# Attention before two expert layers on one core: the first pairs' maxima for both heads at once, and the reciprocal's correction inside the bank of the sums

## The chip, the cores and the metric

The kernel runs on one core of a Trainium2 chip. The metric is the device time of one execution in microseconds (us); the time of a kernel is the median of its runs. A profile is one further execution, recorded by the hardware profiler. Engines: PE is TensorE (matmuls), DVE is VectorE, ACT is ScalarE, POOL is GpSimd, SP issues most of the DMAs. PSUM is the memory that PE writes, in banks; SBUF is the working memory.

## What is computed

Three stages follow each other: attention over 4 x 8 heads (1152 positions, head size 64; the queries are first averaged in pairs, which leaves 576), a layer with `g = h*cos(h)`, and a layer with eight experts, one of which is chosen for each token. Only attention matters here:

```python
q_pool = q.reshape(B, H, S // factor, factor, D).mean(axis=3)
scores = scale * np.matmul(q_pool, k.transpose(0, 1, 3, 2))
scores = scores - np.max(scores, axis=-1, keepdims=True)
attn = np.exp(scores)
attn = attn / (np.sum(attn, axis=-1, keepdims=True) + 1e-09)
return np.matmul(attn, v).astype(np.float32)
```

## The kernel before

Attention works on 16 pairs of heads; the two heads of a pair lie on partitions 0 to 63 and 64 to 127. The queries of a pair are handled in two halves (`hq`) of 288, the keys in nine blocks (`j`) of 128. For every pair these steps run:

- `load`, `loadv`: DMAs of queries, keys and values. `qadd` (L248) adds neighbouring queries, on POOL. `kh`, `qh`, `qt` (L254 to L264, ACT) make rounded copies for the maxima.
- The maxima. `mx` (L273, L276) multiplies a tile of 128 queries (`t` = 0 to 3, and the last 64 queries of both heads as `t` = 4) by a third of the keys (`g`), for both heads at once, into one PSUM tile of two halves; `red` (L302, L305, DVE) reduces both halves in one instruction. There are 14 such tiles in a pair, and one buffer for them (the pool "x"; at the very start two more are lent by the scores' pool). For the second part of pair 0 (tiles `t` = 3 and 4) and for all of pair 1 the kernel does it in another way: `mx1` (L285, L287) fills one half of a tile that stays, in turn the first and the second half, and `red1` (L296) reduces that half.
- `mneg` (L314) joins the thirds and negates, `pmr` (L319) transposes, `mrow` (L324) copies, `mset` (L331, L333) puts the result into the rows `MR` by four DMAs. For the first part of pair 0 `pmq` (L340) and `mput` (L343) do that without a DMA.
- The scores. `s` (L349, L351) computes one block's scores with the maximum taken off, for both heads; `exp` (L355, ACT) takes their exponentials; `es` (L362, POOL) adds up the nine exponentials of a half, eight additions; `pv` (L368) multiplies by the values.
- The end of a half. `ob` (L372) copies the output out of PSUM, negated; `sum` (L377) sums the exponentials over the keys into a bank of PSUM; `ln` (L381) and `rcp` (L385), both on ACT, make a first reciprocal `r0` as exp(-ln(sum)); `nr1` (L389) and `nr2` (L392), both on DVE, correct it by one step: nr = (sum + 1e-9)*r0, then (nr - 2)*r0. `norm` (L400, POOL) multiplies.

Beside these run 32 conversions of weights for the next stage: `cload`, `cabs` (L413, ACT), `c1` to `c4` (L417 to L426, DVE), `chi` (L430, ACT), `clo` (L433, DVE), `cst`. They work in the pool "m", a single PSUM bank, which the transposed maxima and the sums use too, one after the other.

The order is not that of loops. `steps` lists every step with a wished time in units (a pair is 6 units), an engine, a cost, what it reads and writes, and a buffer; `plan` then builds the order of all five queues: it runs through simulated time and always takes, among the steps that an engine may take next (those wished for no later than `AHEAD` units after its first open one), the one with the least sum of its wished time, `WAIT` times its wait, and `SWITCH` when PE would change between its two layouts. For two buffers in turn it only knows what `steps` says: `mx1` waits there for the reduction of its own half alone. The kernel is then issued in the planned order, each engine's queue in that order.

Of the kernel before, what the change touches and what calls it, by code (L numbers as in the profile page):

```python
# [8 lines left out]
F32 = mybir.dt.float32  # L9
# [19 lines left out]
AHEAD = {"PE": 4.5, "DVE": 3.78, "ACT": 3, "POOL": 3.61, "SP": 8.0}  # L29
CHANGE = {COLS: 0.2, ROWS: 0.1}  # L30
EARLY = 4
BEHIND = 1.54
SPREAD = 5.1
WAIT, SWITCH = 6.04, 0.85


def steps(NP, NJ, J):


    P, nx = [], 0  # L40
# [5 lines left out]
    for i in range(NP):  # L46
        b = 6*i
        first = i == 0
        p = -101 if first else b - 10.75
# [8 lines left out]
        for x in whole:  # L58
            c = ((0.67, 0.33)[x] if first else 1)
            at(p + -0.49 + 9*x, "qadd", (i, x), "DVE" if first and not x else "POOL", 1.45*c, [("qr", i, x)] + [("q", i, 0)]*x, [("q", i, x)], None if x else ("q", 3, ("q", i, 0)))  # L60
            at(p + 0.1 + 9*x, "qh", (i, x), "ACT", 0.2 + 0.47*c, [("q", i, x)] + [("qh", i, 0)]*x, [("qh", i, x)], None if x else ("qh", 2, ("qh", i, 0)))
# [3 lines left out]
        at(-4 if first else p + 0.98, "qt", (i,), "ACT", 0.48, [("q", i, whole[-1])], [("qt", i % 2)])  # L65
        parts = ((0, 3), (3, 5)) if first else ((0, 5),)
        for lo, hi in parts:
            p = (-4 if lo else -100) if first else b - 8.47
            for n, (t, g) in enumerate(tiles):
                if lo <= t < hi:  # L70
# [5 lines left out]
                    if lo or i == 1:  # L76
                        for h in range(2) if t < 4 else (0, 1)[:3-g]:
                            half = ("x", nx % 2)
                            at(x, "mx1", (i, t, g, h, nx % 2), ROWS, 0.19, ks + [("xe",)]*(nx > 0), [half] + [("xe",)]*(nx == 0), None if nx else ("x", 1, ("xe",)))
                            at(x, "red1", (i, t, g, h, nx % 2), "DVE", 0.56, [half, ("xe",)], [("mx", i, lo)])  # L80
                            nx += 1
                        continue
                    at(x, "mx", (i, t, g), ROWS, 0.35 if (t, g) == (4, 0) else 0.19, ks, [key], ("s", 2, key) if p == -100 and n % 3 else ("x", 1, key))
                    at(x + 0.08, "red", (i, t, g), "DVE", 0.56 if (t, g) == (4, 2) else 0.96, [key], [("mx", i, lo)])
# [10 lines left out]
        for hq in range(2):  # L95
            for j in range(J):
# [4 lines left out]
                at(m + 0.17, "exp", key, "ACT", 0.65, [("s", *key)], [("e", *key)], ("e", 14, ("e", *key)))  # L101
                if j:
                    at(m + 0, "es", key, *(("DVE", 0.8) if (i, hq) == (NP-1, 1) and j > 4 else ("POOL", 1.45)), [("e", *key)] + [("e", i, hq, 0)]*(j == 1), [("es", i, hq)], ("es", 2, ("es", i, hq)) if j == 1 else None)
                at(m + BEHIND, "pv", key, COLS, 0.486, [("v", i), ("e", *key)], [("o", i, hq)], ("o", 1, ("o", i, hq)) if j == 0 else None)
            m = b + 3*hq + max(3.9, BEHIND + 2.7)
            key = (i, hq)
            at(m + -0.11, "ob", key, "ACT", 0.41, [("o", *key)], [("ob", *key)], ("ob", 2, ("ob", *key)))
            at(m + 0.1, "sum", key, COLS, 0.486, [("es", *key)], [("sum", *key)], ("m", 1, ("sum", *key)))
            at(m + 0.5, "ln", key, "ACT", 0.5, [("sum", *key)], [("ln", *key)], ("ln", 2, ("ln", *key)))
            at(m + 0.46, "rcp", key, "ACT", 0.44, [("ln", *key)], [("r0", *key)], ("r0", 2, ("r0", *key)))  # L110
            at(m + 0.3, "nr1", key, "DVE", 0.46, [("sum", *key), ("r0", *key)], [("nr", *key)], ("nr", 2, ("nr", *key)))
            at(m + 0.6, "nr2", key, "DVE", 0.46, [("r0", *key)], [("nr", *key)])
            at(m + 0.54, "norm", key, "POOL", 0.95, [("nr", *key), ("ob", *key)], [("xT", *key)])
    for n in range(NJ):
        x = 10.76 + 3.01*n if n < 27 else 89 + 1.2*(n - 27)
        at(x - 5, "cload", (n,), "SP", 0.6, (), [("ct", n)], ("ct", 2, ("ct", n)))
        at(x, "cabs", (n,), "ACT", 0.65, [("ct", n)], [("ca", n)], ("m", 1, ("ca", n)))
        for c in range(1, 5):
            at(x + 0, f"c{c}", (n,), "DVE", 0.69, [("ct", n)], [("ca", n)])
        at(x + 0.27, "chi", (n,), "ACT", 0.58, [("ca", n)], [("co", n)], ("co", 2, ("co", n)))  # L120
# [66 lines left out]
def attention(nc, tc, q, k, v, xT, ident, w_in, w_out, ws, x2d, W1):  # L187
# [11 lines left out]
    with ExitStack() as ctx:  # L199
# [78 lines left out]
        def mx1(i, t, g, h, b):  # L278

# [745 lines left out]
```

## Time and profile before

| | us |
|---|---|
| median of 3 runs (1231.37 to 1232.37) | 1232.14 |
| the profiled execution | 1230.01 |
| its span, first to last instruction | 1228.3 |
| PE busy | 1189.6 (97%) |
| DVE busy | 891.7 (73%) |
| ACT busy | 764.0 (62%) |
| POOL busy | 469.1 (38%) |

Busy time is the time in which an engine executes instructions; PE's ends are modelled, so a PE that counts as busy need not be at its peak. POOL's work lies almost wholly in the first 490 us, which is attention; in the later stages PE is the engine that is nearly always busy. The granted TensorE clock is 0.998 on average. The rows below name an instruction by its line, its engine and its tiles, as output<-inputs.

### The profile page before, as it was taken

The numbers are of one execution on the slowest core, as the hardware profiler recorded it, in microseconds if no ns is written. First come the engines' busy times: TensorE is split into PE (matmuls) and PEld (weight loads), VectorE is DVE, ScalarE is ACT, GpSimd is POOL, SyncE is SP. The second block draws the span as 40 slices with busy tenths as digits, with TensorE's granted clock in tenths as the row PEclk, the third lists the DMA queues.
The fourth block names the chain that finished last, engine by engine and source line by source line (L and its number), as shares of the span: only waits on it lengthen the run. The fifth ranks groups of instructions, "written<-read, shape, count | busy, mean of one in ns | idle before, by whom it ended". The sixth has DMA issues, their size and how long they took to land. (4 is left out here: it accounts for less than half of the span.)

```text
span 1228.3 us, 22291 instructions
## 1 busy us (share of the span) xinstructions
PE 1189.6 (97%) x8158; PEld 932.2 (76%) x8158; DVE 891.7 (73%) x1916; ACT 764.0 (62%) x1528; POOL 469.1 (38%) x414
## 2 busy tenths in 40 slices
PE   4799999999999999999999999999999999999997
PEld 2466666666666556989898889889987888888886
DVE  4568887887788767777767767767777877777761
ACT  2266666666666667666566565565575877677751
POOL 2489999999999886000000000000003121112100
PEclk9999999999999999999999999999999999999999
DMA  6034466434433236600000000000047997889710
GB/s 256 18 94 127 157 220 209 152 128 146 143 127 108 89 115 245 259 19 1 18 19 1 19 1 18 19 1 18 26 160 252 398 319 265 273 274 308 265 56 6
DMA packets 70942, 163.73 MB, mean 133 GB/s; under 512 B 7669, under 2 KB 24813, under 8 KB 68784
## 3 DMA queue, kind: packets, MB, share of 16 engines
q1 hardware_dynamic: 66832, 150.92, 35.5%
q0 software_dynamic: 4000, 11.38, 2.6%
q8 instruction: 64, 1.05, 0.3%
q14 instruction: 46, 0.38, 0.1%
HBM read 135.65 MB, written 28.39 MB: 134 GB/s over the span
## 5 line engine op out<-in xcount | busy, mean ns | idle before, releaser
L362 POOL TENSOR_TENSOR es<-es,E 128x576 f32<-128x576 f32 x220 | 313.7, 1426 | 27.4 <-ACT E L355 14.9
L355 ACT ACTIVATE E<-s 128x576 f32<-128x576 f32 x288 | 183.2, 651 | 109.6 <-PE s L351 102.2
L897 PE MATMUL h<-xh,wf 128*128 128x256 f32 x1152 | 231.9, 285 | 0.1
L918 PE MATMUL po<-wf,g 128*128 128x512 f32 x864 | 222.3, 394 | 1.3 <-ACT g L909 0.6
L302 DVE TENSOR_REDUCE MX<-pmx 128x2 f32<-128x768 f32 x177 | 168.7, 956 | 55.8 <-PE pmx L273 55.7
L754 POOL DMA_INDIRECT xg<-x2d,idx x25 | 26.9, 1075 | 465.5 <-ACT ar L902 388.8
L349 PE MATMUL s<-Q,K 64*128 64x288 f32 x1152 | 193.8, 419 | 1.5 <-ACT E L355 1.5
L897 PEld LDWEIGHTS h<-xh,wf 128*128 128x128 f32 x1152 | 188.1, 191 | 6.6 <-issue 1.8
L918 PEld LDWEIGHTS po<-wf,g 128*128 128x128 f32 x864 | 153.4, 189 | 28.1 <-ACT g L909 1.3
L743 DVE TENSOR_TENSOR w<-raw,w 128x1024 fp32r<-128x1024 f32 x128 | 154.6, 1220 | 22.2 <-ACT w L742 20.2
L897 PE MATMUL h<-xl,wf 128*128 128x256 f32 x576 | 163.2, 283 | 0.0
L368 PE MATMUL o<-E,vt 128*64 128x288 f32 x1152 | 161.2, 414 | 0.0
L351 PE MATMUL s<-MR,ON 64*128 64x288 f32 x576 | 148.5, 508 | 0.0
L742 ACT CAST w<-raw 128x1024 fp32r<-128x1024 f32 x128 | 132.9, 1052 | 20.5 <-DMA raw<-in_moe_w_dram 11.9
L821 PE MATMUL po<-w,hh 128*128 128x512 f32 x600 | 144.4, 393 | 1.0 <-DVE hh L792 0.6
L821 PEld LDWEIGHTS po<-w,hh 128*128 128x128 f32 x600 | 110.5, 188 | 24.1 <-DVE hh L792 1.5
L906 ACT ACTIVATE ar<-ar 128x256 f32<-128x256 f32 x144 | 60.1, 417 | 96.7 <-DVE ar L905 96.3
L368 PEld LDWEIGHTS o<-E,vt 128*64 128x64 f32 x1152 | 75.2, 136 | 58.2 <-issue 15.3
L349 PEld LDWEIGHTS s<-Q,K 64*128 64x128 f32 x1152 | 96.6, 187 | 25.8 <-ACT E L355 11.5
L897 PEld LDWEIGHTS h<-xl,wf 128*128 128x128 f32 x576 | 110.0, 191 | 3.7
L788 PE MATMUL ph<-xh,w 128*128 128x256 f32 x576 | 109.7, 287 | 1.0 <-ACT xh L715 1.0
L825 POOL DMA_INDIRECT out_dram<-ob,idx x25 | 27.2, 1090 | 201.9 <-ACT ob L824 183.8
(204 smaller groups left out, 1849.2 us busy)
## 6 DMA issues: line engine op xcount, KB each, us to landing
raw<-in_moe_w_dram SPq DMA_DIRECT2D x128, 512.0 KB
wf<-ws SPq DMA_DIRECT2D x16, 1024.0 KB
vt<-in_v_dram SPq DMA_DIRECT2D x16, 576.0 KB
qr<-in_q_dram SPq DMA_DIRECT2D x15, 576.0 KB
K<-in_k_dram SPq DMA_DIRECT2D x15, 576.0 KB
cv_t<-in_moe_w_in_dram SPq DMA_DIRECT2D x16, 512.0 KB
ws<-cv_o SPq DMA_DIRECT2D x32, 256.0 KB
cv_t<-in_moe_w_out_dram SPq DMA_DIRECT2D x16, 512.0 KB
```

The lines of the kernel that those rows point to most:

```text
L302: nc.vector.reduce_max(out.rearrange("p (w g) -> p w g", g=3)[:, 2*t:2*t+2, g], p[:, :, :KG], axis=AX.X)
L349: nc.tensor.matmul(p[:, h, :NQ], lhsT=T["k", i][R[h], j*128:(j+1)*128], rhs=T["q", i][R[h], qs], start=True, stop=False)
L351: nc.tensor.matmul(p[:, h, :NQ], lhsT=ON[R[h]], rhs=MR[i % 3][R[h], qs], start=False, stop=True)
L355: nc.scalar.activation(e, T.pop(("s", i, hq, j))[:, :, :NQ], AF.Exp, scale=1.0/16)
L362: (nc.vector if (i, hq) == (NP-1, 1) and j > 4 else nc.gpsimd).tensor_add(T["es", i, hq], T["e", i, hq, 0] if j == 1 else T["es", i, hq], ...
L368: nc.tensor.matmul(T["o", i, hq][64*h:64*h+64], lhsT=T["v", i][:, h, j], rhs=T["e", i, hq, j][:, h], start=(j == 0), stop=(j == J-1))
L742: nc.scalar.copy(w[:, 0], t)
L743: nc.vector.tensor_sub(w[:, 1], t, w[:, 0])
L788: nc.tensor.matmul(ph, lhsT=wt[k][:, a, m*128:(m+1)*128], rhs=x[k//2][y][:, k % 2], start=(c == 0), stop=(c == 3*KC-1))
L821: nc.tensor.matmul(po, lhsT=hs[m][:, y, q*128:(q+1)*128], rhs=wt[4 + m//2][:, a, (m % 2)*512:(m % 2)*512+512], start=(c == 0), stop=(c == ...
L897: nc.tensor.matmul(h, lhsT=w[:, a, k*128:(k+1)*128], rhs=x[k//2][y][:, k % 2], start=(n == 0), stop=(n == 3*KC-1))
L918: nc.tensor.matmul(pos[c][t], lhsT=g[:, y, t*128:(t+1)*128], rhs=W1[f][:, b, 512:], start=(f == 0 and i == 0), stop=(f == FT-1 and i == 2))
```

## The change

Four things are done. The steps `mx1` and `red1` are gone, so that pair 0's second part and pair 1 use `mx` and `red` like all other pairs. `nr1` writes its result into the bank of the sums, over the sum, and `nr2` reads it from there and writes `nr` in SBUF. In `steps` `nr1` no longer writes `nr` but `sum`, so that the bank is released after `nr2`. And the planner's constants and some wished times are others. Nothing else of the kernel changes.

```diff
...
-AHEAD = {"PE": 4.5, "DVE": 3.78, "ACT": 3, "POOL": 3.61, "SP": 8.0}
+AHEAD = {"PE": 4.54, "DVE": 4.7, "ACT": 3, "POOL": 3.07, "SP": 8.0}
...
-BEHIND = 1.54
+BEHIND = 1.39
...
-WAIT, SWITCH = 6.04, 0.85
+WAIT, SWITCH = 6.19, 0.7
...
-    P, nx = [], 0
+    P = []
...
-        p = -101 if first else b - 10.75
+        p = -101 if first else b - 12.5
...
-            at(p + -0.49 + 9*x, "qadd", (i, x), "DVE" if first and not x else "POOL", 1.45*c, [("qr", i, x)] + [("q", i, 0)]*x, [("q", i, x)], None if x else ("q", 3, ("q", i, 0)))
+            at(p + -0.71 + 9*x, "qadd", (i, x), "DVE" if first and not x else "POOL", 1.45*c, [("qr", i, x)] + [("q", i, 0)]*x, [("q", i, x)], None if x else ("q", 3, ("q", i, 0)))
...
-        at(-4 if first else p + 0.98, "qt", (i,), "ACT", 0.48, [("q", i, whole[-1])], [("qt", i % 2)])
+        at(-4 if first else p + 1.96, "qt", (i,), "ACT", 0.48, [("q", i, whole[-1])], [("qt", i % 2)])
...
-            p = (-4 if lo else -100) if first else b - 8.47
+            p = (-4 if lo else -100) if first else b - 8.37
...
-                    if lo or i == 1:
-                        for h in range(2) if t < 4 else (0, 1)[:3-g]:
-                            half = ("x", nx % 2)
-                            at(x, "mx1", (i, t, g, h, nx % 2), ROWS, 0.19, ks + [("xe",)]*(nx > 0), [half] + [("xe",)]*(nx == 0), None if nx else ("x", 1, ("xe",)))
-                            at(x, "red1", (i, t, g, h, nx % 2), "DVE", 0.56, [half, ("xe",)], [("mx", i, lo)])
-                            nx += 1
-                        continue
...
-                    at(x + 0.08, "red", (i, t, g), "DVE", 0.56 if (t, g) == (4, 2) else 0.96, [key], [("mx", i, lo)])
+                    at(x + -0.65, "red", (i, t, g), "DVE", 0.56 if (t, g) == (4, 2) else 0.96, [key], [("mx", i, lo)])
...
-                at(m + 0.17, "exp", key, "ACT", 0.65, [("s", *key)], [("e", *key)], ("e", 14, ("e", *key)))
+                at(m + 0.43, "exp", key, "ACT", 0.65, [("s", *key)], [("e", *key)], ("e", 14, ("e", *key)))
...
-                    at(m + 0, "es", key, *(("DVE", 0.8) if (i, hq) == (NP-1, 1) and j > 4 else ("POOL", 1.45)), [("e", *key)] + [("e", i, hq, 0)]*(j == 1), [("es", i, hq)], ("es", 2, ("es", i, hq)) if j == 1 else None)
+                    at(m + -0.1, "es", key, *(("DVE", 0.8) if (i, hq) == (NP-1, 1) and j > 4 else ("POOL", 1.45)), [("e", *key)] + [("e", i, hq, 0)]*(j == 1), [("es", i, hq)], ("es", 2, ("es", i, hq)) if j == 1 else None)
...
-            m = b + 3*hq + max(3.9, BEHIND + 2.7)
+            m = b + 3*hq + max(3.62, BEHIND + 2.7)
...
-            at(m + -0.11, "ob", key, "ACT", 0.41, [("o", *key)], [("ob", *key)], ("ob", 2, ("ob", *key)))
-            at(m + 0.1, "sum", key, COLS, 0.486, [("es", *key)], [("sum", *key)], ("m", 1, ("sum", *key)))
-            at(m + 0.5, "ln", key, "ACT", 0.5, [("sum", *key)], [("ln", *key)], ("ln", 2, ("ln", *key)))
-            at(m + 0.46, "rcp", key, "ACT", 0.44, [("ln", *key)], [("r0", *key)], ("r0", 2, ("r0", *key)))
-            at(m + 0.3, "nr1", key, "DVE", 0.46, [("sum", *key), ("r0", *key)], [("nr", *key)], ("nr", 2, ("nr", *key)))
-            at(m + 0.6, "nr2", key, "DVE", 0.46, [("r0", *key)], [("nr", *key)])
-            at(m + 0.54, "norm", key, "POOL", 0.95, [("nr", *key), ("ob", *key)], [("xT", *key)])
+            at(m + 0, "ob", key, "ACT", 0.41, [("o", *key)], [("ob", *key)], ("ob", 2, ("ob", *key)))
+            at(m + 0.15, "sum", key, COLS, 0.486, [("es", *key)], [("sum", *key)], ("m", 1, ("sum", *key)))
+            at(m + 0.75, "ln", key, "ACT", 0.5, [("sum", *key)], [("ln", *key)], ("ln", 2, ("ln", *key)))
+            at(m + 0.74, "rcp", key, "ACT", 0.44, [("ln", *key)], [("r0", *key)], ("r0", 2, ("r0", *key)))
+            at(m + 0.21, "nr1", key, "DVE", 0.46, [("r0", *key)], [("sum", *key)])
+            at(m + 0.64, "nr2", key, "DVE", 0.46, [("r0", *key), ("sum", *key)], [("nr", *key)], ("nr", 2, ("nr", *key)))
+            at(m + 0.42, "norm", key, "POOL", 0.95, [("nr", *key), ("ob", *key)], [("xT", *key)])
...
-        x = 10.76 + 3.01*n if n < 27 else 89 + 1.2*(n - 27)
+        x = 10.21 + 3.04*n if n < 27 else 89 + 1.2*(n - 27)
...
-            at(x + 0, f"c{c}", (n,), "DVE", 0.69, [("ct", n)], [("ca", n)])
-        at(x + 0.27, "chi", (n,), "ACT", 0.58, [("ca", n)], [("co", n)], ("co", 2, ("co", n)))
+            at(x + 0.18, f"c{c}", (n,), "DVE", 0.69, [("ct", n)], [("ca", n)])
+        at(x + 0, "chi", (n,), "ACT", 0.58, [("ca", n)], [("co", n)], ("co", 2, ("co", n)))
...
-        def mx1(i, t, g, h, b):
-
-            if "xe" not in T:
-                T["xe"] = ps_x.tile([128, 2, 512], F32, tag="x", name="pmx")
-            p = T["xe"][:, b, :KG]
-            KH, QH = T["kh", i], T["qh", i]
-            if t < NT4:
-                nc.tensor.matmul(p, lhsT=QH[R[h], t*128:(t+1)*128], rhs=KH[R[h], g*KG:(g+1)*KG], start=True, stop=True)
-            else:
-                nc.tensor.matmul(p, lhsT=QT[i % 2], rhs=KH[:, (g+h)*KG:(g+h+1)*KG], start=True, stop=True)
-
-        def maxima(i):
+        def red(i, t, g):
+            p = T.pop(("x", i, t, g))
...
-            return T["mx", i]
-
-        def red1(i, t, g, h, b):
-            o = 24+g+h if t == NT4 else 3*(2*t+h)+g
-            nc.vector.reduce_max(maxima(i)[:, o:o+1], T["xe"][:, b, :KG], axis=AX.X)
-
-        def red(i, t, g):
-            p = T.pop(("x", i, t, g))
-            out = maxima(i)
+            out = T["mx", i]
...
+            nc.vector.scalar_tensor_tensor(T["sum", i, hq], T["sum", i, hq], 1e-9, T["r0", i, hq], op0=ALU.add, op1=ALU.mult)
+
+        def nr2(i, hq):
...
-            nc.vector.scalar_tensor_tensor(T["nr", i, hq], T["sum", i, hq], 1e-9, T["r0", i, hq], op0=ALU.add, op1=ALU.mult)
-
-        def nr2(i, hq):
-            nc.vector.scalar_tensor_tensor(T["nr", i, hq], T["nr", i, hq], 2.0, T["r0", i, hq], op0=ALU.subtract, op1=ALU.mult)
+            nc.vector.scalar_tensor_tensor(T["nr", i, hq], T["sum", i, hq], 2.0, T["r0", i, hq], op0=ALU.subtract, op1=ALU.mult)
...
```

## Rows read from the trace of the kernel before

**Rows 1.** Windows by stage: length, busy us of each engine (instructions), granted clock, DMA

```profile
30.00:60.00 30.00, 23.40 (x131) 13.37 (x133) 16.15 (x33) 9.24 (x16) 13.85 (x10) 1.00 0.06 18
...
150.00:400.00 250.00, 249.46 (x1980) 154.94 (x1978) 201.44 (x276) 168.02 (x300) 236.62 (x192) 1.00 0.47 155
```

**Rows 2.** POOL's timeline: start, us, instruction; the first `es` of pairs 0, 1, 13

```profile
37.05 1.43 POOL L362 TENSOR_TENSOR es<-E 128x576 f32<-128x576 f32 x1 [18.34 <-ACT E L355]
...
73.20 1.46 POOL L362 TENSOR_TENSOR es<-E 128x576 f32<-128x576 f32 x1
...
400.28 1.45 POOL L362 TENSOR_TENSOR es<-E 128x576 f32<-128x576 f32 x1 [0.36 <-ACT E L355]
```

**Rows 3.** Waits from 19 to 58 us, and from 150 to 400: total, times, longest

```profile
POOL es L362 <- ACT E L355: 25.4, 5, 18.3
...
POOL es L362 <- ACT E L355: 6.1, 18, 0.4
```

**Rows 4.** Timeline of the start, several engines: start, us, instruction [idle before it <-releaser]

```profile
19.12 0.69 PE L285 MATMUL pmx<-KH,QH 64*128 64x384 f32 x2 [1.59 <-ACT QH L260]
...
20.16 0.85 PE L351 MATMUL s<-MR,ON 64*128 64x288 f32 x2
...
22.26 0.68 PE L285 MATMUL pmx<-KH,QH 64*128 64x384 f32 x1 [0.65 <-DVE MX L296]
...
23.60 0.68 PE L285 MATMUL pmx<-KH,QH 64*128 64x384 f32 x1 [0.65 <-DVE MX L296]
...
35.60 0.15 DVE L314 TENSOR_REDUCE mneg<-MX 128x3 f32<-128x9 f32 x1
...
57.82 0.18 DVE L314 TENSOR_REDUCE mneg<-MX 128x9 f32<-128x27 f32 x1
...
61.19 0.51 SPq L333 DMA_DIRECT2D MR<-mrow  x1
```

**Rows 5.** Groups by line and form to 540 us: count, busy us, mean ns, idle before

```profile
L302 DVE TENSOR_REDUCE MX<-pmx 128x2 f32<-128x768 f32 x177 | 168.7, 956 | 55.8 <-PE pmx L273 55.7
...
L392 DVE SCALAR_TENSOR_TENSOR nr<-nr,r 128x288 f32<-128x288 f32 x32 | 28.2, 883 | 0.6
...
L426 DVE SCALAR_TENSOR_TENSOR cv_a<-cv_t,cv_a 128x512 int32<-128x512 int32 x32 | 22.1, 691 | 0.7
...
L296 DVE TENSOR_REDUCE MX<-pmx 128x1 f32<-128x384 f32 x36 | 19.4, 555 | 20.0 <-PE pmx L285 15.2 <-PE pmx L287 4.8
...
L389 DVE SCALAR_TENSOR_TENSOR nr<-psum,r 128x288 f32<-128x288 f32 x32 | 14.5, 452 | 17.5 <-ACT r L385 17.4
```

**Rows 6.** Timeline of PE, two whole tiles of pair 2 in a row

```profile
70.76 0.45 PE L273 MATMUL pmx<-KH,QH 64*128 64x384 f32 x2
...
72.28 0.43 PE L273 MATMUL pmx<-KH,QH 64*128 64x384 f32 x2
```

**Rows 7.** Timeline of POOL, three `es` beside an `nr2` and three without one

```profile
267.85 4.51 POOL L362 TENSOR_TENSOR es<-es,E 128x576 f32<-128x576 f32 x3
...
286.17 4.39 POOL L362 TENSOR_TENSOR es<-es,E 128x576 f32<-128x576 f32 x3
```

**Rows 8.** Timeline of DVE, ACT and PE around the bank of the sums, one pair

```profile
255.72 0.46 DVE L389 SCALAR_TENSOR_TENSOR nr<-psum,r 128x288 f32<-128x288 f32 x1 [0.75 <-ACT r L385]
...
269.65 1.43 DVE L392 SCALAR_TENSOR_TENSOR nr<-nr,r 128x288 f32<-128x288 f32 x1
...
277.23 0.69 DVE L433 TENSOR_TENSOR cv_o<-cv_a,cv_o 128x512 fp32r<-128x512 f32 x1 [0.65 <-ACT cv_o L430]
...
256.21 0.64 ACT L413 ACTIVATE cv_a<-cv_t 128x512 f32<-128x512 f32 x1
...
270.12 0.64 ACT L413 ACTIVATE cv_a<-cv_t 128x512 f32<-128x512 f32 x1
...
281.24 0.71 PE L377 MATMUL psum<-es,ones 128*64 128x288 f32 x4
```

**Rows 9.** Timeline of PE at the end of attention

```profile
478.52 0.71 PE L377 MATMUL psum<-es,ones 128*64 128x288 f32 x4 [0.46 <-DVE cv_o L433]
```


## The prediction

> **What bounds the kernel now.** I read the windows by stage first, then POOL's own timeline, then the waits, then single instructions of the start. In the windows [rows 1] the reader is to see two regimes. From 30 to 60 us no engine is full: PE is busy for 23.40 of 30 us, DVE for 16.15, POOL for 13.85. In the long stretch of attention, 150 to 400 us, PE counts as busy throughout and POOL is for 236.62 of 250 us, while DVE has 201.44 and ACT 168.02. So DVE time alone is worth nothing in the long stretch; time is to be had at the start, or on POOL.
>
> POOL's timeline says it exactly [rows 2]. The first `es` addition of a pair marks the pace: pair 1 at 73.20 us, pair 13 at 400.28, so 327.08/12 = 27.26 us per pair, while the very first `es` comes at 37.05. Whatever makes pair 1's additions start earlier, at the same pace, makes attention end earlier, and PE goes on to the next stage in program order. The waits [rows 3] show POOL idle for 25.4 us between 19 and 58 us for want of exponentials, but for 6.1 only in the 250 us of the long stretch.
>
> The timeline of the start shows why [rows 4]. A half's matmul begins at 22.26 (0.68 us), its reduction takes 0.56 [rows 5], and the next half's matmul begins at 23.60: 1.34 us per half, one after the other. The code has two halves of one tile to work in, but the second is not filled while the first is reduced. Nine halves of pair 0 run from 19.12 until the `mneg` at 35.60, the 27 halves of pair 1 until the `mneg` at 57.82, and the reductions idle 20.0 us for the matmuls [rows 5].
>
> **Part 1: both heads together in pair 0's last and pair 1's maxima.** 36 half matmuls with 36 reductions (19.4 us) become 19 tiles with 17 reductions of 0.956 and 2 of about 0.556 us, 17.4 us of DVE [rows 5]. What counts is the chain. A whole tile, where the chain already has that form, takes 72.28 - 70.76 = 1.52 us from matmul to matmul [rows 6]; with the slow matmuls of the start 0.68 + 0.96 and two short gaps, 1.73. Pair 0's five tiles: 4 x 1.73 + 1.34 (a single half) = 8.3 us. The planner now sees one buffer, finds PE waiting for it and puts score groups between, which cost up to 1.4 us each there (until 21.0, after the half at 19.12 [rows 4]), so I take 10 in place of 16.5. Pair 1's 14 tiles: 13 x 1.52 + 1.1 = 20.9 in place of 22.2. The chain then ends at 19.1 + 10 + 20.9 = 50 instead of 57.8.
>
> After it come the transposition, `mrow` and four DMAs, the last issued 3.9 us after `mneg` begins (57.82 to 61.70 [rows 4]); for the landing I allow the 1.9 us that the kernel's own planner reckons with. So pair 1's scores can start at 56 and its first `es` at 58, 15 us ahead of 73.20, if pair 0 is out of the way. On POOL it is: with score groups let in between, the first `es` can come near 23 us, and 16 additions of 1.43 with some small steps are 25 us. On PE too: it does one pair's whole work in 27.26 us later, and five more tiles at 0.45 add 2.3, while 19 to 56 us are 37. Bounds: if every tile has to wait for 1.95 us (27.26/14, the pace of the later pairs) the chain ends at 56 and 2 us are won; with no score group in the way of the chain, 17. I take 11, nearer to the upper end because both engines have room. What is late next is then the four DMAs of the maxima.
>
> **Part 2: `nr1` writes into the bank, `nr2` reads it there.** The old second step has both inputs in SBUF and takes 883 ns; its neighbour `nr1`, with one input in PSUM, takes 452, and an instruction that reads and writes PSUM 691 for 512 columns [rows 5], so 288 columns should not exceed 0.46. I take 0.45 for both steps: 32 x 0.43 = 13.8 us of DVE, on the path for nothing, as DVE idles for 20% of the long stretch; without that cover it would be up to 0.86 us per pair. But POOL has to do with the old `nr2`: three `es` around one take 4.51 us, three without it 4.39 [rows 7]. That is 0.11 us per `nr2`, 0.22 per pair, 3 us over 13 pairs; PE stands back to back as well [rows 1], so I count -1.5, between -3 and 0. The Trainium skill ("SBUF — State Buffer", section "Who interferes with whom") says that a DVE instruction with two SBUF inputs and a GpSimd instruction that reads SBUF exclude each other, the second blocking until the first is done. For DVE the trace agrees (1.43 us for one `nr2` [rows 8]), for POOL it shows 0.11 us; by that rule the whole `nr2` could be POOL's loss, which would be rival (d).
>
> The price: the one bank ("m") of sums, transposed maxima and conversions is now held until `nr2` ends. Before, a conversion's `cabs` starts at 256.21, as `nr1` ends at 256.18 [rows 8]; it will start 0.45 us later, and the exponentials behind it on ACT's queue with it. In the pair's other half `cabs` starts at 270.12, while `nr2` ends at 271.08: 0.96 later, or nothing if `nr2` follows `nr1` at once. The bank has room for it: of the 3.3 us between that conversion's end (277.92) and the next sum (281.24) only the short transposition uses a part. So 0 in the long stretch. At the tail sums and conversions follow each other in the bank, and PE's sum at 478.52 waits for a conversion [rows 9]: three sums at 0.45 there, +1, between 0 and +1.5.
>
> **Part 3: the new constants.** They re-sort all five queues. `qadd`, `qh`, `kh` and `qt` move 1 to 2 of the planner's units (27.26/6 = 4.5 us each) ahead; their loads don't, and still lead by over 8 units, 37 us; on POOL `qadd` stays one addition per pair, and `q`'s three buffers hold it behind the scores of three pairs before. No instruction and no DMA is added. The order can give back POOL's 6.1 us of waits in 9 pairs, 0.67 per pair, or double them: 12 x 0.67 = 8 us either way. I take 0.
>
> **Sum.** -11 - 1.5 + 1 + 0 = -11.5 us. The profiled execution took 1230.0 us (span 1228.3 and 1.7 around it), which gives 1218.5; it lay 2.1 below the median of 1232.14, so 1220.5 in that measure.
>
> **The rivals.** (a) The chain shortens but pair 0's own work is not done earlier: the 15.4 us from pair 1's `mneg` to its first `es` (57.8 to 73.2) stay, or score groups stretch every tile to 1.95 us. Then 2 to 8 us are won, 5 in the middle: 1227. For it speaks that PE's matmuls are slow at the start, against it that PE idles for 6.6 of the 30 us [rows 1].
> (b) Slower: the bank becomes the bound. If its empty time (most of 3.3 us) is of no use, as the sum behind it has a time of its own, conversions start 0.5 + 0.96 = 1.46 us later in each pair, and exponentials behind them; 13 pairs make 19 us, and 1220.5 + 19 = 1239. It decides once the bank's cycle is longer than POOL's 27.26. For it: `cabs` follows `nr1` by 0.03 us at one of the two sums; against it: those 3.3 us, and that `nr2` can follow `nr1` at once.
> (c) The re-sorting gives the gain back, POOL waiting twice as often over the whole stretch, +8 to +11: 1231, no change.
> (d) POOL lost the whole 0.46 us of each `nr2`: 26 of them in the stretch that POOL sets, 26 x (0.46 - 0.11) = 9 us more, 1211. Rows 7 speak against it. That the second step isn't shortened at all is possible too, but moves the sum by 1.5 only.
>
> **Chances.** Forecast 0.60, (a) 0.17, (b) 0.10, (c) 0.08, (d) 0.05. More than 0.2% faster (2.5 us, about what a measurement of this kernel can tell from no change) are the forecast, (d) and most of (a): 0.79; the same 0.11; slower 0.10. The range reaches down to 1208 (17 us at the start, 3 from POOL and some of the order's; past (d)) and up to 1231, with (a) and (c) in it and (b) left out.
>
> **What would show it.** Right: the lines 285, 287 and 296 gone, pair 1's reductions about 1.5 us apart, the first `es` near 23 us, pair 1's near 62 or before, a pace of 27.0 to 27.3 us, `nr2` at 0.45 us with little spread, three `es` always 4.4 us. Wrong: pair 1's first `es` still at 70 or later; a pace above 27.6 with `cabs` waiting for `nr2` and POOL for exponentials behind it; or a longer way than before from the last `es` to the next stage.

## The result and the profile after

The changed kernel takes 1212.53 us (median of 4 runs, 1210.33 to 1213.97) beside 1232.25 for the kernel before: a ratio of 0.984, 95% interval 0.9823 to 0.9857, 18 to 22 us less. The forecast was 1220.5 with a range of 1208 to 1231: faster as said and inside the range, but by some 20 us where the sum had 11.5.

Where it went is read from two profiled executions, 1228.3 and 1212.3 us of span, 16.0 apart. (The profiled one of after was the highest of its four runs, and that of before, 1230.01, lay below all four of its own, so the traces show less than the medians.) Four marks cut the span: pair 1's first `es`, pair 13's first `es`, and the first and the last matmul of the next stage's first layer (`h`).

| stretch, us | before | after | difference |
|---|---|---|---|
| to pair 1's first `es` | 73.20 | 58.80 | -14.40 |
| to pair 13's | 327.08 | 328.33 | +1.25 |
| to the first `h` | 79.36 | 74.66 | -4.70 |
| to the last `h` | 422.9 | 424.2 | +1.3 |
| to the end | 325.8 | 326.3 | +0.5 |

So the start gave nearly all of it, the end of attention the rest, and the 12 pairs between gave nothing together. First the windows of after, which answer to [rows 1]:

```profile
30.00:60.00 30.00, 30.00 (x225) 17.79 (x225) 20.02 (x27) 15.90 (x30) 21.74 (x17) 1.00 0.23 75
150.00:400.00 250.00, 250.00 (x1981) 155.37 (x1983) 193.50 (x276) 170.87 (x305) 235.11 (x193) 1.00 0.46 146
```

From 30 to 60 us PE is now busy throughout (23.40 before) and POOL for 21.74 us (13.85). In the long stretch DVE has 7.9 us less to do; the other engines have moved by less than 3. POOL's timeline of after, for [rows 2] and [rows 7] (the row at 297.23 has a wait that before does not have):

```profile
25.55 1.43 POOL L337 TENSOR_TENSOR es<-E 128x576 f32<-128x576 f32 x1 [7.00 <-ACT E L330]
...
58.80 1.45 POOL L337 TENSOR_TENSOR es<-E 128x576 f32<-128x576 f32 x1 [3.65 <-ACT E L330]
...
273.69 4.41 POOL L337 TENSOR_TENSOR es<-es,E 128x576 f32<-128x576 f32 x3
...
297.23 0.94 POOL L375 TENSOR_TENSOR xT<-ob,nr 128x128 f32<-128x128 f32 x2 [0.41 <-DVE nr L367]
...
387.13 1.46 POOL L337 TENSOR_TENSOR es<-E 128x576 f32<-128x576 f32 x1
```

The three `es` at 273.69 take 4.41 us, as they did without an `nr2` beside them. Pair 0 begins 11.5 us earlier, pair 1 14.4; the pace is (387.13 - 58.80)/12 = 27.36 us per pair, 27.26 before. The start's timeline of after, for [rows 4]:

```profile
18.97 0.69 PE L266 MATMUL pmx<-KH,QH 64*128 64x384 f32 x2 [1.59 <-ACT QH L253]
...
29.01 0.16 DVE L289 TENSOR_REDUCE mneg<-MX 128x3 f32<-128x9 f32 x1
...
36.20 0.44 PE L266 MATMUL pmx<-KH,QH 64*128 64x384 f32 x2
...
37.72 0.42 PE L266 MATMUL pmx<-KH,QH 64*128 64x384 f32 x2
...
51.24 0.18 DVE L289 TENSOR_REDUCE mneg<-MX 128x9 f32<-128x27 f32 x1
```

Pair 0's five tiles take 29.01 - 18.97 = 10.0 us with the score groups between them (10 forecast), two of pair 1's tiles follow each other by 1.5 us, and its `mneg` comes at 51.24 (50 forecast, 57.82 before). So 6.6 us of the 14.4 are won ahead of this `mneg`, all of them in pair 0: from one `mneg` to the next it takes 22.2 us (29.01 to 51.24), as it did before (35.60 to 57.82). The other 7.8 are won behind it: from pair 1's `mneg` to its first `es` it is now 7.6 us instead of 15.4. The groups of DVE and ACT up to 540 us, for [rows 5]:

```profile
L277 DVE TENSOR_REDUCE MX<-pmx 128x2 f32<-128x768 f32 x192 | 183.3, 958 | 77.2 <-PE pmx L266 76.6
...
L363 DVE SCALAR_TENSOR_TENSOR psum<-psum,r 128x288 f32<-128x288 f32 x32 | 14.7, 461 | 12.9 <-ACT r L360 12.9
...
L367 DVE SCALAR_TENSOR_TENSOR nr<-psum,r 128x288 f32<-128x288 f32 x32 | 14.5, 453 | 1.5
```

`nr2` takes 453 ns where it took 883, as forecast. The price stands in the waits of after from 150 to 400 us, for [rows 3] and [rows 8]:

```profile
POOL es L337 <- ACT E L330: 4.1, 9, 1.1
POOL xT L375 <- DVE nr L367: 2.9, 7, 0.4
...
ACT cv_a L388 <- DVE nr L367: 18.6, 18, 1.1
```

`cabs`, the first step of a conversion (L388 now), waits 18 times, about 1 us each, for `nr2`, which now holds the bank. At the end of attention, for [rows 9], a sum waits for `nr2` where one waited 0.46 for a conversion:

```profile
461.79 0.39 PE L872 MATMUL h<-xh,wf 128*128 128x256 f32 x1
...
464.99 0.71 PE L352 MATMUL psum<-es,ones 128*64 128x288 f32 x4 [0.68 <-DVE nr L367]
```

### The profile page after: what moved, and what is told of

Same layout as the page of the kernel before. It is cut to its first block, busy times and chain, and to the rows that moved or that the text cites. A ratio compares the mean times of both kernels' runs of the same rounds, so it can differ in the third digit from the quotient of the medians.

```text
span 1212.3 us, 22307 instructions
## 1 busy us (share of the span) xinstructions
PE 1185.7 (98%) x8158; PEld 930.5 (77%) x8158; DVE 877.5 (72%) x1899; ACT 764.5 (63%) x1528; POOL 467.1 (39%) x414
## 5 line engine op out<-in xcount | busy, mean ns | idle before, releaser
L277 DVE TENSOR_REDUCE MX<-pmx 128x2 f32<-128x768 f32 x192 | 183.3, 958 | 77.2 <-PE pmx L266 76.6
```

The source lines that it names most:

```text
L277: nc.vector.reduce_max(out.rearrange("p (w g) -> p w g", g=3)[:, 2*t:2*t+2, g], p[:, :, :KG], axis=AX.X)
```

## The experiments

Three things are changed: the maxima (M), the bank of `nr1` and `nr2` (B) and the constants (C). With the two kernels of the case, six more give all eight combinations. Then one with the working place of `nr2` alone changed, one that mends the halves in another way, and four that follow up what the eight showed. The marks are read as above; a median is set against runs of the kernel before on the same chip (medians of 1230.75 to 1231.24, and 1232.25 beside after).

| kernel | parts | median (runs) | ratio, interval | pair 1's `es` | pair 13's | first `h` | last `h` |
|---|---|---|---|---|---|---|---|
| before | | 1232.25 | | 73.20 | 400.28 | 479.64 | 902.5 |
| e1_maxima | M | 1216.49 (4) | 0.9868 [0.9848, 0.9887] | 60.00 | 389.28 | 467.57 | 890.4 |
| e2_bank | B | 1237.61 (4) | 1.0046 [1.0029, 1.0063] | 75.08 | 403.36 | 482.74 | 910.6 |
| e3_both | MB | 1222.89 (4) | 0.9927 [0.9911, 0.9944] | 58.24 | 386.53 | 467.32 | 895.2 |
| e4_const | C | 1233.42 (10) | 1.0013 [1.0003, 1.0023] | 77.16 | 409.17 | 484.04 | 908.5 |
| e5_sbuf | MC | 1213.25 (4) | 0.985 [0.9834, 0.9867] | 57.44 | 386.97 | 461.67 | 886.3 |
| e6_halves | BC | 1232.1 (10) | 1.0018 [1.0008, 1.0027] | 72.86 | 403.05 | 479.17 | 903.3 |
| after | MBC | 1212.53 (4) | 0.984 [0.9823, 0.9857] | 58.80 | 387.13 | 461.79 | 886.0 |
| e7_operand | after, `nr2` in SBUF | 1217.09 (4) | 0.9884 [0.9866, 0.9901] | 57.52 | 388.44 | 463.07 | 887.8 |
| e8_tail | MB, conversions closer | 1224.28 (4) | 0.9955 [0.9938, 0.9972] | 60.70 | 389.01 | 470.8 | 897.5 |
| e9_nr2 | after, `nr2` wished earlier | 1217.11 (5) | 0.9886 [0.9869, 0.9903] | 58.55 | 387.88 | 464.80 | 889.5 |
| e10_two_tiles | before, halves as two tiles | 1219.03 (4) | 0.9908 [0.9889, 0.9926] | 61.90 | 389.03 | 468.4 | 891.3 |
| e11_tables | e3, Sin behind the last Exp | 1221.83 (5) | 0.9934 [0.992, 0.9947] | 58.75 | 387.07 | 467.97 | 893.4 |
| e12_copies | e1, first copies later | 1216.45 (4) | 0.9882 [0.9867, 0.9897] | 57.75 | 386.85 | 464.53 | 887.4 |

An interval of four runs is about 4 us wide, and the unchanged stages behind the last `h` took between 324.9 and 328.7 us in these profiles. So what is under 2 us in a median is not told apart. Distances between marks are the finer measure: among kernels whose queues have the same order up to there (before and e10; e1 and e12; e3, e8 and e11) the way from pair 1 to pair 13 differs by 0.2 us at most. Pair 1's own mark is not: it is 2.3 us apart in e1 and e12, and 2.5 in e3 and e8. From 26 to 30 us the same matmuls of the scores take 765 ns on the average in the later one of each and 428 to 455 in the earlier; why stays open.

**The eight combinations.** M alone takes out `mx1` and `red1`, B alone changes the two steps (with the lines of `nr1` and `nr2` as in the change), C alone is every number of the change's diff on the old steps; the others are unions of these. The cores of the three edits, M first:

```diff
-                    if lo or i == 1:
...
-                            nx += 1
-                        continue
```

```diff
-            at(m + 0.3, "nr1", key, "DVE", 0.46, [("sum", *key), ("r0", *key)], [("nr", *key)], ("nr", 2, ("nr", *key)))
-            at(m + 0.6, "nr2", key, "DVE", 0.46, [("r0", *key)], [("nr", *key)])
+            at(m + 0.3, "nr1", key, "DVE", 0.46, [("r0", *key)], [("sum", *key)])
+            at(m + 0.6, "nr2", key, "DVE", 0.46, [("r0", *key), ("sum", *key)], [("nr", *key)], ("nr", 2, ("nr", *key)))
```

```diff
-AHEAD = {"PE": 4.5, "DVE": 3.78, "ACT": 3, "POOL": 3.61, "SP": 8.0}
+AHEAD = {"PE": 4.54, "DVE": 4.7, "ACT": 3, "POOL": 3.07, "SP": 8.0}
...
-        p = -101 if first else b - 10.75
+        p = -101 if first else b - 12.5
...
```

> The kernel before with one edit: pair 0's second part and pair 1 use mx and red (both heads at once); old constants, old nr1/nr2. Theory (the start's serial chain of halves was the loss): pair 1's first es between 58 and 62 us instead of 73.2, pace still 27.2 to 27.4 us per pair, 1217 to 1221 us. Rival A (the new order made by the constants is what counts): within 3 us of 1232. Rival B (the second step of the reciprocal, through POOL's share in it, is what counts): 1232.

> The kernel before with one edit: nr1 writes into the bank of the sums and nr2 reads it there, in the code and in the planner's list; old constants, old halves. Theory: three es take 4.39 us each time, but PE stands back to back too, so 1229 to 1232 us, pair 1's first es unchanged near 73. Rival B: POOL gets 0.2 us per pair and more back and the pace falls below 27.0: 1220 or less. Rival C (the bank held longer slows the conversions and the exponentials behind them): above 1235.

> The kernel before with both edits of the code (both heads at once, and the bank), old constants. Theory: the two are independent, so e1's time less 0 to 3 us: 1215 to 1220; the rest down to the changed kernel's 1212.5 is the constants' (the tail). Rival A: still above 1228.

> The changed kernel with both edits of the code taken back: the halves and the old nr1/nr2 as before, only the new constants and wished times. Theory: the start is as slow as before (pair 1's first es at 71 to 75), the tail from pair 13 on is some 4 us shorter: 1226 to 1230 us. Rival A: 1218 or less.

> The changed kernel with the old nr1/nr2 (through SBUF) in code and planner's list; both heads at once and new constants stay. If the terms simply added (maxima -14.8, constants +2.2 from the first four runs) 1218.7 us. Theory now (the constants are made for the longer hold of the bank; with the bank they gain, without it they lose): 1216 to 1220, and the three es around an nr2 take 4.5 us again. Rival (the bank always costs its 6 us): about 1206, below the changed kernel.

> The changed kernel with the halves of before (mx1, red1) put back; bank and new constants stay. Theory (the start's chain is independent of the rest): the changed kernel plus 13 to 16 us, 1225 to 1229, pair 1's first es at 71 to 75. Rival A (the new order mends the start by itself): below 1220.

Only e1 came out as expected in the main, half a us below its range. e2, e3, e4 and e6 were slower than their theories had them, by 3 to 6 us, and e5 faster by 3; in e2 the time of the rival C came, but not by its way (below).

Measured against the kernel before: M is worth -14.75 us by itself and -14.7 on top of B; on top of C it is -20.2, on top of B and C -19.6. B costs 6.4 us with the old constants, with and without M, and gives about 1 with the new ones (e4 to e6 -1.3, e5 to after -0.7, neither told apart from nothing). C costs 2.2 alone and gives 3.2 on top of M, 5.5 on top of B, 10.4 on top of M and B. So the maxima carry the change, the bank alone would have been a loss, and the constants are good only with the rest. (Medians of different chips are compared here where M or B is set on top of C, or C on top of another part.)

Most of B's loss lies where attention meets the next stage: from the first to the last `h` e2 and e3 take 427.9 us, before and e1 422.9 and 422.8. ACT's timeline of e2 there, with the matmul that waited:

```profile
488.90 1.28 ACT L906 ACT_TABLE_LOAD   x1
...
490.63 1.28 ACT L385 ACT_TABLE_LOAD   x1
491.93 0.44 ACT L385 ACTIVATE r<-ln 128x288 f32<-128x288 f32 x1
...
492.69 1.28 ACT L906 ACT_TABLE_LOAD   x1
...
493.24 0.39 PE L897 MATMUL h<-xh,wf 128*128 128x256 f32 x1 [3.15 <-DVE ar L908]
```

The longer hold of the bank made the planner put the last conversion between pair 15's two sums. The last sum comes late, its `rcp` (L385, an Exp) falls between the next stage's first two Sin (L906), and ACT changes its table three times, 1.28 us each, where before and after load one table there. PE waits for the chain behind those Sin, and behind that wait the granted clock is lower. The window of e2:

```profile
490.00:500.00 10.00, 6.85 (x35) 6.11 (x35) 5.35 (x17) 7.84 (x17) 2.84 (x15) 0.83 0.98 398
```

PE is busy for 6.85 of 10 us and the clock, 1.00 in the windows ahead, is 0.83 on the average; in the windows of after from 460 to 510 us it is 1.00 throughout.

**Half tiles as tiles of their own.** e10 keeps the steps, the constants and the planned order of before; the two halves in turn are only two tiles of one bank each, no longer halves of one tile. The core of the edit (the rest opens and closes the pools for it):

```diff
-            if "xe" not in T:
-                T["xe"] = ps_x.tile([128, 2, 512], F32, tag="x", name="pmx")
-            p = T["xe"][:, b, :KG]
+            T["xe", b] = p = xpool("a_ps_h", 2).tile([128, 512], F32, tag="h", name="pmx")
+            p = p[:, :KG]
```

> The kernel before with its planned order of all queues as it is; only the two halves that mx1 and red1 use are two tiles of their own (one bank each) instead of two halves of one tile. Theory (the serial chain of the start was the shared tile, for which every half waits for the last reduction of either): a half takes 0.6 to 0.9 us instead of 1.34, pair 0's second mneg comes at 24 to 28 us instead of 35.6, pair 1's first es between 58 and 64: 1216 to 1223 us. Rival (the slow matmuls of the start, or the order itself, set the chain): 1.2 us and more per half, within 3 us of 1231.

It takes 1219.03 us, 12 less than before, as the theory has it (only pair 0's `mneg`, at 29.28, comes 1.3 us later than forecast). The timeline of e10 at the start, and its group of half reductions:

```profile
22.06 1.02 DVE L306 TENSOR_REDUCE MX<-pmx 128x1 f32<-128x384 f32 x2 [0.49 <-PE pmx L295]
...
29.28 0.15 DVE L324 TENSOR_REDUCE mneg<-MX 128x3 f32<-128x9 f32 x1
...
46.52 0.18 DVE L324 TENSOR_REDUCE mneg<-MX 128x9 f32<-128x27 f32 x1
...
61.90 1.44 POOL L372 TENSOR_TENSOR es<-E 128x576 f32<-128x576 f32 x1
```

```profile
L306 DVE TENSOR_REDUCE MX<-pmx 128x1 f32<-128x384 f32 x36 | 18.9, 554 | 8.3 <-PE pmx L295 5.3 <-PE pmx L297 2.2
```

The same 36 reductions of the same 0.55 us now mostly follow in twos without a gap; they idle 8.3 us instead of 20.0 [rows 5], pair 0's `mneg` comes at 29.28 instead of 35.60 [rows 4], pair 1's 17.2 us later instead of 22.2, and pair 1 starts 11.3 us earlier. So the order was not what cost the time; the halves of one tile were waited for as if they were one, and that alone cost some 12 us. A whole tile in one go has nothing to lose by it, so this is what M removes too. But M wins in another place: with the order of before, e10 has all of its gain ahead of pair 1's `mneg` and keeps the 15.4 us behind it (46.52 to 61.90), while M, which re-sorts the queues, wins 5.4 ahead of it and 7.8 behind (52.43 and 60.00 in e1). How much of M's gain is the re-sorting wasn't tried.

**The place of `nr2`.** e7 is after, with the same order in every queue, but with `nr1` and `nr2` in SBUF as before:

```diff
-            nc.vector.scalar_tensor_tensor(T["sum", i, hq], T["sum", i, hq], 1e-9, T["r0", i, hq], op0=ALU.add, op1=ALU.mult)
+            T["nr", i, hq] = sm.tile([128, NQ], F32, tag="nr", name="nr")
+            nc.vector.scalar_tensor_tensor(T["nr", i, hq], T["sum", i, hq], 1e-9, T["r0", i, hq], op0=ALU.add, op1=ALU.mult)
...
-            nc.vector.scalar_tensor_tensor(T["nr", i, hq], T["sum", i, hq], 2.0, T["r0", i, hq], op0=ALU.subtract, op1=ALU.mult)
+            nc.vector.scalar_tensor_tensor(T["nr", i, hq], T["nr", i, hq], 2.0, T["r0", i, hq], op0=ALU.subtract, op1=ALU.mult)
```

> The changed kernel's own order of all queues (the planner's list is untouched), but nr1 writes an SBUF tile and nr2 works on it in SBUF as before: only where the value lies between the two steps differs, and the bank is free after nr1 in fact. Theory (POOL loses 0.11 us beside each nr2, DVE 0.43): pace slower by up to 0.3 us per pair, 0 to +4 us against the changed kernel: 1213 to 1217. Rival (the operand's place is worth the gain by itself, POOL being shut out for the whole step): +8 us or more, above 1220. Rival (the earlier release of the bank outweighs it): below 1211.

Its median is 4.6 us above that of after, just above what the theory allowed, and the intervals don't touch. The pace is (388.44 - 57.52)/12 = 27.58 us, 0.22 more, which is 2.6 us over the 12 pairs; as pair 1 is 1.3 us ahead (within what this mark varies by), the first `h` comes 1.3 us later. The group of `nr2` in e7, two waits of e7 from 60 to 400 us, and the rows of POOL and of one `nr2`:

```profile
L367 DVE SCALAR_TENSOR_TENSOR nr<-nr,r 128x288 f32<-128x288 f32 x32 | 33.1, 1034 | 0.5
```

```profile
PE pmx L266 <- DVE MX L277: 1.4, 4, 0.5
...
POOL xT L375 <- DVE nr L367: 7.5, 19, 0.4
```

```profile
274.52 4.42 POOL L337 TENSOR_TENSOR es<-es,E 128x576 f32<-128x576 f32 x3
...
280.42 4.40 POOL L337 TENSOR_TENSOR es<-es,E 128x576 f32<-128x576 f32 x3
...
284.00 1.14 DVE L367 SCALAR_TENSOR_TENSOR nr<-nr,r 128x288 f32<-128x288 f32 x1
...
285.21 0.94 POOL L375 TENSOR_TENSOR xT<-ob,nr 128x96 f32<-128x96 f32 x2 [0.39 <-DVE nr L367]
```

In this order `nr2` takes 1034 ns, 581 more than in the bank. PE waits 1.4 us for reductions, which stand behind `nr2` in DVE's queue (after has no such wait in that stretch), and `norm` waits for `nr2` 19 times instead of 7. The `es` are hardly longer (mean 1417 ns, 1415 in after from 60 to 400 us). What POOL loses is a wait: all 24 `nr2` of e7 in this stretch begin during an `es` and end 0.31 to 0.32 us after it, whatever they took (here at 285.14, the `es` at 284.82), and where `norm` stands right behind that `es` (20 times) it begins 0.39 to 0.40 us after it, where an `es` in its place begins after 0.08. In before the same holds of the 25 `nr2` there, but each time another `es` stands next, which begins as always and takes 0.1 us longer; so there the old `nr2` costs POOL 0.1 us each. Between the two profiles it is 4.2 us: 1.3 less to pair 1, 2.6 more in the pairs, 0.5 more in the next stage's first layer and 2.4 more behind it, where the code is the same and the profiles vary by more than that.

**Earlier `nr2`.** e9 is after with `nr2` wished right behind `nr1` (which the planner then does in 30 of 32 cases), so that the bank is free sooner:

```diff
-            at(m + 0.64, "nr2", key, "DVE", 0.46, [("r0", *key), ("sum", *key)], [("nr", *key)], ("nr", 2, ("nr", *key)))
+            at(m + -0.5, "nr2", key, "DVE", 0.46, [("r0", *key), ("sum", *key)], [("nr", *key)], ("nr", 2, ("nr", *key)))
```

> The changed kernel with one wished time: nr2 at m - 0.5 instead of m + 0.64, by which it stands right behind nr1 in DVE's order in 30 of 32 cases (18 before). Theory (the waits of cabs for nr2, 25.8 us on ACT, are beside the path, as PE and POOL stand back to back): those waits fall by half or more and the time stays within 2 us, 1211 to 1214. Rival (the longer hold of the bank costs time in every pair): 1209 or less.

The waits of e9 on ACT from 60 to 470 us:

```profile
ACT cv_a L388 <- DVE nr L367: 6.6, 6, 1.1
```

They fall from 25.8 us (25 times in after, same stretch) to 6.6, and the kernel is 4.6 us slower, neither the same, as the theory had it, nor faster: the first `h` comes 3.0 us later, 2.3 of it lost between pair 13's first `es` and the first `h`. The way from pair 1 to pair 13 is 1.0 us longer without these waits. So the 18.6 us that `cabs` waits in the long stretch lie beside the path, as the prediction's zero says; what moves the time is how the planner sorts the rest, the end above all.

**Two tries at the end of attention that missed, and a third by halves.** e8 is e3 with the last five conversions wished 0.9 units apart instead of 1.2, to have them out of the sums' way:

```diff
-        x = 10.76 + 3.01*n if n < 27 else 89 + 1.2*(n - 27)
+        x = 10.76 + 3.01*n if n < 27 else 89 + 0.9*(n - 27)
```

> The kernel with both edits of the code and old constants (e3), and one number more: the last five conversions are wished for 0.9 units apart instead of 1.2, which puts the last conversion ahead of the last two sums in the planned order; up to the last sums of pair 14 the order is that of e3. Theory (e3's 6 us over e1 are the late last sum: ACT loads its function tables three times instead of once, PE waits 3.2 us and runs its matmuls slower after it): one table load at the change of stage, 1216 to 1219 us. Rival (the longer hold of the bank costs it all along): as e3, 1221 to 1225.

The median, 1224.28, is that of the rival, and of e3. No conversion stands between the last two sums any more, but the three table loads stayed (475.13, 476.86 and 481.70 us) and PE waited 3.7 us in two parts for the same `ar`. The granted clock is 1.00 from 470 to 500 us all the same, and from the first to the last `h` it takes 426.7 us: so a loss of 3.8 us there, of e3's 5.0, can come without the lower clock. e11 separates the loads in another way: it is e3 with the next stage's first two Sin kept behind attention's last `rcp` on ACT.

```diff
...
-            last["act"] = nc.scalar.activation(r, r, AF.Sin, scale=0.5).ins
+            with tc.issue_after(L["rcp"]) if c == 0 and f < 2 else ExitStack():
+                last["act"] = nc.scalar.activation(r, r, AF.Sin, scale=0.5).ins
```

> The kernel with both parts of the change and the constants of before (1222.9 us), with one addition: the first two Sin of the next stage's first chunk stand behind attention's last Exp of the reciprocal on ACT. Nothing else of the attention moves. Theory (the 6 us that the bank costs under the old constants are the table loads between the Sin and the late Exp, 3 x 1.28 us, and the clock that falls while PE waits for them): one table load is left, near 474 us; PE's wait for DVE's first ar, some 3 us in the run without the addition, goes; the median falls by 2.5 to 5 us, to 1218-1220.4. Rival (the late last sum itself is the cost, the loads lie beside it): the loads go, the first chunk starts no earlier, and the median stays at 1222-1224.

ACT's timeline, PE's wait from 462 to 500 us, and a window of e11:

```profile
474.37 0.44 ACT L360 ACTIVATE r<-ln 128x288 f32<-128x288 f32 x1
...
474.83 1.28 ACT L882 ACT_TABLE_LOAD   x1
476.13 0.72 ACT L882 ACTIVATE ar<-ar 128x256 f32<-128x256 f32 x2
```

```profile
PE h L872 <- DVE ar L884: 2.4, 1, 2.4
```

```profile
480.00:490.00 10.00, 10.00 (x67) 9.10 (x66) 7.61 (x22) 5.98 (x16) 0.32 (x2) 1.00 1.02 428
```

One load is left and the clock of this window is 1.00 (0.87 in e3), but PE still waits 2.4 us instead of 3.2. From the first to the last `h` it is 425.4 us, 2.5 below e3's 427.9 and 2.5 above before. The median, 1221.83, misses the 1218 to 1220.4 of the theory and is not told apart from e3's. So the trace gives half of B's cost to the loads and the clock. The other half I take to be the late last sum itself, behind which the Sin now wait; no run shows that by itself.

e12 asks what the constants give behind pair 13. In before and e1 the next stage's first two copies (L715 and L690, the `xh`) stand among pair 13's exponentials on ACT. ACT's timeline of before, a row not shown ahead:

```profile
404.62 1.14 ACT L715 CAST xh<-xT 128x512 fp32r<-128x512 f32 x2 [2.49 <-POOL Q L248]
```

e12 is e1 with these copies behind the last exponential of pair 15's first half:

```diff
...
-        split_x(xs[0], xT[0])
+        with tc.issue_after(L["exp"]):
+            split_x(xs[0], xT[0])
```

> The kernel with the maxima of both heads alone and the constants of before (1216.5 us), with one addition: the next stage's first two copies, which stand on ACT among pair 13's exponentials and wait there 2.37 us for the last Q of POOL, stand behind the last exponential of pair 15's first half. No other queue changes. Theory (this wait is most of what the new constants give behind pair 13): pair 13's first half takes 13 us instead of 15.5, the next stage begins 2 to 3 us earlier, the median is 1213.5-1214.5, beside 1213.25 of the same kernel with the new constants. Rival (ACT has time there, and PE and POOL catch up by the end of pair 15; or the copies cost as much where they now stand): the first half of pair 13 is shorter but the next stage begins within 0.7 us of the run without the addition, and the median stays at 1216-1217.

The copies then run at 451.04 and 452.65 us without a wait. From pair 13's first `es` to pair 14's it takes 27.38 us (28.62 in e1, 25.97 in after), but from pair 15's to the first `h` 23.29 (22.32 in e1). What is won is 1.2 us where 2.5 were thought, and 1.0 of it is paid back where the copies now stand; the median is that of e1. (That its first `h` comes 3.0 us before e1's is for the most part older: its profile is 2.3 us ahead at pair 1 already, where nothing of the kernel differs.) The rival holds: this wait isn't what the constants give.

What C does can be put in place, if not taken apart. The way from pair 13's first `es` to the first `h` is shorter with C in all four comparisons: by 4.5 us (before, e4), 3.3 (e2, e6), 3.6 (e1, e5) and 6.1 (e3, after). Up to pair 13 it takes back 8.9 us where the serial halves are and B isn't (e4, of which 4.0 are there by pair 1); the 2.3 that it seems to give where M is without B (e5) lie at pair 1, within what that mark varies by. In the next stage's first layer it takes back B's loss (424.2 in after, 427.9 in e3), but costs 1.6 to 1.8 us where B isn't (424.5 in e4 and 424.6 in e5, 422.9 and 422.8 without C). Which of the constants do that wasn't tried.

## Why the prediction was right, and where it was off

- **What bounds.** Right. Most of the gain lies in the start, as read from [rows 1 to 4], and the pace behind it stayed within 0.1 us, a little above the 27.0 to 27.3 named as a sign.
- **Part 1, the maxima: -11 taken, -14.4 in the trace, -14.75 alone by the median.** The mechanism is the one forecast, and most steps came out nearly as counted (10.0 us for pair 0's tiles, `mneg` at 51.24, 7.6 us from there to the first `es`, 8 counted). But 1.34 us per half was the period of pair 0 only: pair 1's 27 halves took 0.82 each on the average, and its 14 tiles saved nothing (22.2 us, 20.9 counted). The mis-sized step is "I take 11": the working before it had pair 1's first `es` at 58, 15 us earlier, and it came at 58.80; the 11 were a middle towards the bound of tiles stretched to 1.95 us, though PE's and POOL's idle time, counted in the same place, spoke for the full 15. e10 shows the cause that the prediction read from the 1.34 us period alone.
- **Part 2, the port: -1.5 taken.** The duration was right (453 ns), and so was the row on POOL: of the 175 additions es<-es,E from 60 to 400 us the longest took 1517 ns before and takes 1434 now, the mean 1428 and 1415. The pace went from 27.26 to 27.36 all the same, but it has all parts of the change in it. From pair 1 to pair 13 M costs 2.2 us (before to e1), B gives 1.0 (e1 to e3), and the constants on top nothing (e3 to after). B gives 1.0 to 1.8 there in three of the four comparisons and costs 1.2 in the fourth (before to e2), and in the fixed order of e7 the place of `nr2` is worth 2.6. So -1.5 was about right for B; what the sum left out is M's 2.2, a price of the new order (e10, with the order of before, has 327.1 us there as before has). The way is another than forecast as well: in e7 POOL loses by `norm` waiting for `nr2`, not by longer `es`.
- **The bank: 0 in the long stretch, +1 at the tail.** The zero was right (e9, and the gain of B in the pairs), with the waits where the prediction had put them. The tail was mis-sized: "three sums at 0.45" prices the wait by its own length, but with the old constants the hold re-sorts the last conversion, and that costs 6.4 us by the median (e2, e3), 5.0 of it in the first layer. In after nothing of it is left.
- **The constants: 0 taken, between 8 either way.** Mis-sized: -3.2 on M, -5.5 on B, +2.2 alone, and -10.4 on M and B, beyond the 8. Taking all constants together as noise around nothing left out what they do once the other parts are in; they bring the -4.70 at the end of attention (-6.1 from e3 to after).
- **The rivals.** (a) and (c) fell with the start and the pace. (b), the bank as the bound, is refuted for the pairs; its sign was right for B alone, at the transition. (d) fell: POOL did not lose a whole `nr2`; an `es` behind one took 0.1 us longer, and a `norm` behind one in e7 began 0.31 later. On the Trainium skill ("SBUF — State Buffer", section "Who interferes with whom"), by which of the two instructions the second blocks until the first is done: for DVE e7 agrees (1034 ns against 453, and none of the 24 ended before the `es` that it met), for POOL the measurement decides, 0.1 us on an `es` and not 0.46.

The sum missed by 8.0 us. In the trace it is 4.5 (-11.5 against -16.0): 3.4 more than forecast at the start, 5.7 at attention's end (+1 against -4.7), less 2.75 in the pace (-1.5 against +1.25) and 1.85 in the stages behind, which were counted at nothing. The other 3.5 are how the two profiled runs stand to their medians. So the start was forecast by its mechanism; that the whole lies inside the range owes also to the range's 23 us and to luck: on top of M the bank cost 6.4 us and the constants gave 10.4, where the sum had -0.5 and 0 for them.

## What to carry to other kernels

Two halves of one tile that are used in turn can still be waited for as one: look in the timeline whether the second matmul begins while the first reduction runs (here 1.34 us per half in pair 0 and 0.82 on the average in pair 1, where e10 has 0.64), and give each half a tile of its own or use the whole at once. When a kernel's order comes from a planner with tuned constants, an edit, its costs in the planner and the constants are one change: the bank edit alone cost 6.4 us and about nothing with its constants. Where one stage ends and the next begins, look for functions of ACT from both stages in one queue. And before a mark of one profile is trusted, look how far it lies apart in two kernels that have the same order up to it.

## What was not expected of the hardware

- A table change takes 1.28 us on ACT each time, and a late Exp between two Sin makes three of them; behind PE's wait for their chain, 3.15 us, the granted clock was 0.83 on the average of 10 us (e2), and 0.87 in e3; in e11, with a wait of 2.4 us, it stayed at 1.00. In e11 the Exp before the load ends at 474.81 us, and the Sin begins 0.02 us after the load. The Trainium skill ("ScalarE: Activation LUTs", section "What ACT_TABLE_LOAD costs") has 1.28 us for the load, which agrees, and some 1.38 us of drain beside it, which these rows do not show.
- `nr2` with both inputs in SBUF, on 288 columns, took 0.48 and 1.43 us in one pair of before, on the average 883 ns in before and 1034 in e7, with the same work; in the bank it is 453 with hardly any spread (446 to 458). What is fixed in SBUF is its end: from 60 to 400 us all 25 of before and all 24 of e7 began during an `es` of POOL and ended 0.31 to 0.32 us after that `es`.
- Kernels with equal code behind attention differ there: from the last `h` to the end 324.9 to 328.7 us in the 14 profiles. One profile is no measure for a part that is worth 2 us.
